# Attention with a new written order: other durations in the planner, padded queries in weight memory, eleven exp buffers

## The chip, the cores and the metric

One NeuronCore of one Trainium2 chip runs the whole program. The metric is the device time of one execution in microseconds (us). The kernel before took 1060.55 us, the median of three runs (1060.35 to 1061.62).

Engines: TensorE (PE, matrix products; PEld is its weight loading), VectorE (DVE), ScalarE (ACT), GpSimd (POOL), SyncE (SP, which here only issues DMAs). All work on SBUF; results of TensorE land in PSUM.

## The reference, cut to what matters

Three layers follow each other. The change touches the first one only.

```
q, k rotated by position (RoPE), batch 4, heads 8, seq 576, head_dim 64
scores = q k^T / 8 ; attn = softmax(scores) ; y = attn v        (fp32)
x = y as 2304 rows of 512
x = (sigmoid(x wg) * (x wv)) wo                                 (gated layer, 512 -> 1536 -> 512)
expert of each row by argmax of its logits; x = p * (relu(x w1[e]) w2[e])   (8 experts)
```

## The kernel before, in words

**Pairs and tiles.** Two heads are worked on together: 16 pairs `p`, each with nine tiles `t` of 128 query rows (four for each head and one that holds the last 64 rows of both heads); `T = 9 p + t`. All products are done with a number split into a high and a low part of the type fp32r, and the products of the parts added.

**One pair.** `plan_loads` (L321) loads raw q and raw k with their half-swapped copies (`sa<-in_qk`, L328), one DMA for q (half 0) and one for k (half 1), and `v` (L338). `plan_prep` (L418) prepares pairs 2 to 15: multiply by the cosine and sine tables for a half ("rope", L162, 128 x 1152), add the two products ("rot", L160), copy out the high part ("hi", L152 on ScalarE or L154 on GpSimd), subtract it to get the low part ("lo", L437), and then 14 DMAs (`cp`, L455) bring the parts into the layout that the products need: `q2`, `kh` (in tile `sb`), `qd` and `qz`. `qz` is the "padded query": the high part of one head's queries with the other 64 partitions zero. Pairs 0 and 1 take another way (`plan_direct`, L358), mostly without DMAs.

The raw tile and the tile of the parts (both in `sa`) exist once. So the load of a half for pair p+1 waits for "lo" of pair p, "hi" of pair p+1 waits for all copies of pair p, and "lo" of pair p also waits for the last scores of pair p-2, whose place it takes (`q2`, `kh`, `kl`, `qz` exist twice).

**One tile** (`plan_tile`, L474): scores on TensorE into PSUM ("s", L183, two PSUM tiles); VectorE copies them out to an exp buffer `e` and takes the row minimum ("tsa", L193); ScalarE does the exponential in place with the row sum (L205); TensorE transposes it (L237); ScalarE copies the high part out ("hi" of the tile, `pth`, L267) and VectorE the low part (`ptl`, L271). `transpose5` (L252) does the last 64 columns for several tiles at once. An exp buffer comes free when both transposes of its tile are done; there are `E_BUFS = 8`. Four times a pair the products with `v` follow ("value", L284), a copy by ScalarE (`xv`, L292) and an add by VectorE (`xy`, L301). Once a pair the reciprocal row sums go through DRAM (`rw`, L498; read back by `recip_rows`, L226) and the result is normalised ("rm", `normalise`, L231). The reads of pair p wait for "rm" of pair p-1.

**What sets the order.** Every instruction of attention is added to a `Plan` with an engine, a cost in us, what it depends on and a due time. `Plan.order` (L52) runs through time: the engine that can start first takes, of what is ready by the plan's own account, the operation with the lowest due time. `LAT` is added to the end of an operation until another engine sees it. All DMAs together are one engine "DMA" that does one transfer after the other, and each has an issue on "SP" (0.62 us below a size of 0.5, else 0.46) ahead of it. What results is the fixed program order of each engine: on the chip an engine waits at the head of its queue when what it needs isn't there, even where later work is ready. The due times are the tables `PR` (preparation) and `OFF` (tiles); the tables `LO`, `VLO`, `ROPE`, `RM`, `HI`, `VHI` name the pairs whose operation of that kind runs on another engine than usual (usual: low part of q or k on VectorE, low part of v on GpSimd, rope and rot on GpSimd, normalisation on GpSimd, high parts on ScalarE).

**Around it.** While attention runs, the three matrices of block 0 of the gated layer's weights are converted from double words (`filler`). `Gated.early` (L726) starts the first gate products in attention's PSUM, and `Gated.opening` makes a plan of its own from the plan's last times. `add_weights` (L624) makes the tiles for converted weights: index 0 and 1 (tag `wr`) before attention, 2 and 3 after it. During attention index 0 is filled; of index 1 only parts are used by `early`, at the end.

Of the kernel before, what the change touches and what calls it, by code (L numbers as in the profile page):

```python
# [8 lines left out]
F32R = mybir.dt.float32r  # L9
# [12 lines left out]
TPP = 9  # L22
E_BUFS = 8
PT_BUFS = 3
# [7 lines left out]
class Plan:  # L32
# [3 lines left out]

    LAT = {"PE": 0.25, "SP": 0.65, "DMA": 1.0}

# [68 lines left out]
class Attention:  # L107
    def __init__(self, tc, pool, xpool, psum_s, psum_t, psum_v, qk, v, rope, ident, xt, rows):
# [12 lines left out]
        self.kl = [t([128, S], F32R, f"kl_{i}") for i in range(2)]  # L121
        self.qd = [t([128, 128], F32R, f"qd_{i}") for i in range(2)]
        self.qz = [t([128, 2, 512], F32R, f"qz_{i}") for i in range(2)]
        sa = xpool.tile([128, 7 * S], F32R, name="sa", tag="sa", bufs=1)
        self.raw = f32(sa[:, 0:4 * S]).rearrange("p (a s) -> p a s", a=4)
        self.hqk = sa[:, 4 * S:7 * S].rearrange("p (a s) -> p a s", a=3)
        self.hq, self.hk = self.hqk[:, 0:2], self.hqk[:, 2]
        sb = xpool.tile([128, 4 * S + 4 * 640], F32R, name="sb", tag="sb", bufs=1)
        kh = sb[:, 0:4 * S].rearrange("p (i x s) -> p i x s", i=2, x=2)
        q2 = sb[:, 4 * S:].rearrange("p (i x s) -> p i x s", i=2, x=2)  # L130
        self.q2, self.kh = ([a[:, i] for i in range(2)] for a in (q2, kh))
        self.xv = t([128, 320], F32, "xv")
# [53 lines left out]
    def evac_scores(self, T):  # L186
        ps = self.s.pop(T)
        e = self.pool.tile([128, 2, SH], F32, name="e", tag="e", bufs=E_BUFS)
        p, t = divmod(T, TPP)
        if t == 0:  # L190
            self.stat[p] = self.pool.tile([128, 3, TPP], F32, name="st", tag="st", bufs=ST_BUFS)
# [129 lines left out]
    def plan_loads(self, p, load_rope=None, load_const=None):  # L321
# [8 lines left out]
        for half in (1, 0) if p == 0 else (0, 1):  # L330
            for n, cols in enumerate(self.cuts(p, half)):
                size = 1.64 * (cols.stop - cols.start) / S
                self.dma(("load", p, half, n), size, ld(half, cols), [("lo", p - 1, half)], at)
                if p == 0 and half == 1:
                    self.dma(("rope", n), size, lambda cols=cols: load_rope(cols), [], at)
        if p == 0:
            self.dma("const", 1.05, load_const, [], at)
        self.dma(("loadv", p), 0.82, lambda: nc.sync.dma_start(out=self.vraw, in_=self.v[b, hp]), [("vlo", p - 1)], at)  # L338

    def plan_v(self, p):  # L340
# [4 lines left out]
        eng = self.VHI.get(p, "ACT")  # L345
        self.op(("vhi", p), eng, {"ACT": 0.57, "POOL": 0.72}[eng], lambda eng=eng: self.copy(eng, vv[:, :, 0], self.vraw),
                [("loadv", p)] + prev, pr)
        eng = self.VLO.get(p, "POOL")
        self.op(("vlo", p), eng, {"DVE": 0.669, "POOL": 1.36}[eng], lambda: self.engine(eng).tensor_tensor(
            out=vv[:, :, 1], in0=self.vraw, in1=f32(vv[:, :, 0]), op=ALU.subtract), [("vhi", p)], pr)  # L350
# [7 lines left out]
    def plan_direct(self, p, pr):  # L358
# [7 lines left out]
        for half in (1, 0):  # L366
            j = 2 * half
            for n, c in enumerate(self.cuts(p, half)):
# [21 lines left out]
                for x in range(2):  # L390
                    last = min(c.stop, 512) if x else c.stop
                    cuts = [(c.start, last, 0)] + ([(512, S, 64)] if last < c.stop else [])
                    for a, b, d in cuts:
# [9 lines left out]
                        if a < 512:  # L403
                            if p > 0:
                                self.dma(("qz", *key), 0.4, lambda x=x, i=slice(a, min(b, 512)): nc.sync.dma_start(
                                    out=f32(self.qz[p][r[x], x, i]), in_=f32(q2[r[x], x, i])), [("qhi", *key)], pr + 1.5 + x + n)
# [11 lines left out]
    def plan_prep(self, p):  # L418
# [6 lines left out]
        for j, off in ((0, 0.0), (2, self.PR["k"])):  # L425
# [4 lines left out]
            c = {"DVE": 0.5, "POOL": 1.0}[eng]  # L430
            self.op(("rope", p, j), eng, 2.57 * c, lambda j=j, eng=eng: self.rope_op(eng, j, "both"), [("load", p, half, 0)], base + off)
            self.op(("rot", p, half), eng, 1.36 * c, lambda j=j, eng=eng: self.rope_op(eng, j, "add"), [("rope", p, j)], base + off)
# [4 lines left out]
            self.op(("lo", p, half), eng, {"DVE": 0.669, "POOL": 1.36}[eng], lambda j=j, hi=hi, lo=lo, eng=eng: self.engine(eng).tensor_tensor(  # L437
                out=lo, in0=raw[:, j], in1=f32(hi), op=ALU.subtract), [("hi", p, half)] + before, base + off + self.PR["split"])
# [15 lines left out]
        for n, (half, o, s) in enumerate(cp):  # L454
            self.dma(("cp", p, n), 0.4 if n < 2 or half else 0.2, lambda o=o, s=s: dma(out=f32(o), in_=f32(s)),  # L455
                     [("lo", p, half)] + before, base + 3 * half + 2)
# [7 lines left out]
    KLO = ((0, 0, 0), (0, 1, 1), (1, 0, 0),)  # L464
    LO = dict.fromkeys(((3, 0), (4, 0), (4, 1), (5, 0), (5, 1), (6, 0), (6, 1), (7, 0), (7, 1), (9, 0), (9, 1), (10, 0), (10, 1), (11, 1), (12, 0), (12, 1), (13, 0), (13, 1), (14, 0), (15, 0), (15, 1),), "POOL")
    VLO = dict.fromkeys((1, 5, 8, 13,), "DVE")
    ROPE = dict.fromkeys(((1, 1),), "DVE")
    PR = dict(ahead=-0.74, k=-25.57, split=-30.40, v=-9.46)
    RM = dict.fromkeys((8, 10, 15,), "DVE")
    HI = dict.fromkeys(((2, 0), (3, 0), (3, 1), (5, 1), (7, 1), (8, 1), (11, 1), (12, 1), (14, 0),), "POOL")  # L470
    VHI = dict.fromkeys((0, 2, 3, 11, 12, 14, 15,), "POOL")
    OFF = dict(table=-3.16, xs=781.16, gv=847.57, post=751.36, rr=85.85, rm=56.64, s=11.92, tsa=14.25, exp=3.09, eps=-75.21, rec=-94.73, norm=-14.47, tr=79.75, hi=4.82, lo=18.38, tr5=-12.17, val=102.41, vc=-0.58, va=-66.51)

# [21 lines left out]
    def plan_norm(self, p):  # L495
# [4 lines left out]
        for x, part in reads:  # L500
            self.dma(("rr", p, x, part), 0.1 if part else 0.36, lambda x=x, part=part: self.recip_rows(p, x, part),
                     [("rw", p), ("rm", p - 1)], T + o["rr"])
        eng = self.RM.get(p, "POOL")
        self.op(("rm", p), eng, {"DVE": 0.67, "POOL": 1.36}[eng], lambda: self.normalise(p, eng),
                [("rr", p, *k) for k in reads] + [("va", p, *k) for k in reads], T + o["rm"])
# [28 lines left out]
    def plan_value(self, p, x, u):  # L534
# [11 lines left out]
    def run(self, npairs=B * NP, loads=(None, None), filler=(), tail=None):  # L546
# [64 lines left out]
class Gated:  # L611
# [196 lines left out]
    def opening(self):  # L808
# [65 lines left out]
        def convert(seq, prio, step, free):  # L874
            for n, (f, m) in enumerate(seq):
                dep = [(*seq[n - 2], 5)] if n > 1 else []
                for i, (eng, cost, fn) in enumerate(self.convert(f, m, nc.sync.dma_start)):
# [738 lines left out]
def build(tc, qk, v, rope, cst_in, wg, wv, wo, wg2, bias, mod, w1, w2, out):  # L1616
# [5 lines left out]
    with tc.manual_schedule(), pool("keep") as keep:  # L1622
        cst = keep.tile([128, CSTW], F32, name="cst", tag="cst")
        ident = cst[:, CST["ident"]]
        with pool("wa") as wa:
            with pool("xy") as xyp, pool("conv") as conv, pool("xs") as xs:
                xy = xyp.tile([128, KC, NT], F32, name="xy", tag="xy")
                gated = Gated(tc, words(wg), words(wv), words(wo), xy, wa, conv, xs, ident)
                with pool("att") as att, \
# [48 lines left out]
```

## Time and profile before

| | |
|---|---|
| median of 3 runs | 1060.55 us |
| profiled execution | 1062.35 us, of it 1060.5 us span |
| busy over the span | PE 94%, DVE 63%, ACT 50%, POOL 36% |
| attention | 0 to about 335 us |
| gated layer, routing, experts | after it, to the end |

An engine's busy time is the sum of its instructions' spans; PE's is modelled. A wait is named after what ended it. "SPq" is SyncE's DMA queue, and a DMA in the chain of waits is the time from its issue until what waited for it went on.

### The profile page before, as it was taken

The page shows a single profiled execution, that of the slowest core. Times are in us where ns is not written, and L with a number is a line of the kernel's source. Part 1 is how long each engine was busy: PE and PEld are TensorE (multiplying, and loading weights), DVE is VectorE, ACT ScalarE, POOL GpSimd, SP SyncE. Part 2 cuts the span into 40 slices and gives each one's busy share as a digit, 9 for nine tenths or more (in the row PEclk, how much of TensorE's full clock was granted, in tenths as well). Part 3 has the DMA queues.
Part 4 walks back from the last instruction along what each step waited for, and adds up shares of the span by engine and source line. Part 5 has one row for each costly group of instructions (what it writes and reads, how often), then busy time and mean ns, then how long its engine had stood idle before and what let it go on. Part 6 is the DMA issues. An engine that isn't in the chain of part 4 may idle for free.

```text
span 1060.5 us, 16517 instructions
## 1 busy us (share of the span) xinstructions
PE 994.1 (94%) x6035; PEld 912.6 (86%) x6035; DVE 664.0 (63%) x1179; ACT 532.9 (50%) x1051; POOL 386.3 (36%) x288
## 2 busy tenths in 40 slices
PE   3988889889899999999999999999998899999996
PEld 2888888889899999999999999998875799999995
DVE  8999788879796764544535545532267755555651
ACT  5878787879796622222222212233331554555552
POOL 5788766778520532322322323211142111211111
PEclk9999999999999999999999999999998999999998
DMA  5567766577511320111111101000027867666640
GB/s 190 164 180 185 169 190 165 151 191 199 152 45 52 109 71 22 60 40 40 41 40 40 60 21 60 20 1 1 1 61 233 295 233 233 225 225 220 222 170 24
DMA packets 74137, 127.24 MB, mean 120 GB/s; under 512 B 14447, under 2 KB 37631, under 8 KB 74048
## 3 DMA queue, kind: packets, MB, share of 16 engines
q1 hardware_dynamic: 60128, 108.53, 34.6%
q0 software_dynamic: 3040, 9.70, 2.7%
q10 hardware_dynamic: 10880, 7.87, 2.4%
q8 instruction: 50, 0.82, 0.3%
q14 instruction: 39, 0.32, 0.1%
HBM read 95.65 MB, written 9.77 MB: 99 GB/s over the span
## 4 chain that ended last, share of the span: by engine, by line
PE 52%; issue 17%; DMA 12%; DVE 9%; ACT 4%; POOL 3%; SPq 2%; ACTq 0%; POOLq 0%; DVEq 0%
PE gv L715 28%; PE yo L781 13%; DMA out<-e_y,r_si 5%; DMA sa<-in_qk 4%; PE pv L284 3%; DMA sb<-sa 3%; PE s L183 3%; DVE e L193 2%; SPq L455 2%; PE pt L237 2%; DVE ptl L271 1%; ACT e L205 1%; POOL e_xg L1446 1%; ACT pth L267 1%; PE s L715 1%
## 5 line engine op out<-in xcount | busy, mean ns | idle before, releaser
L724 POOL TENSOR_TENSOR gl<-sg,gh 128x384 fp32r<-128x384 f32 x60 | 64.2, 1070 | 263.3 <-ACT gh L723 263.3
L722 DVE TENSOR_TENSOR sg<-gv,sg 128x384 f32<-128x384 f32 x70 | 39.0, 557 | 140.9 <-PE gv L715 118.9
L205 ACT ACTIVATE e<-e,st 128x576 f32<-128x576 f32 x144 | 112.1, 782 | 8.3 <-DVE e L193 7.5
L1439 DVE TENSOR_TENSOR e_w<-wr,e_w 128x1024 fp32r<-128x1024 f32 x80 | 95.9, 1222 | 28.9 <-ACT e_w L1438 27.1
L183 PE MATMUL s<-sb 128*128 128x288 f32 x320 | 78.1, 335 | 33.5 <-DVE sb L398 14.0
L193 DVE TENSOR_SCALAR_CACHE_REDUCE e<-s 128x576 f32<-128x576 f32 x144 | 105.6, 745 | 2.6 <-PE s L183 2.0
L721 ACT ACTIVATE sg<-gv 128x384 f32<-128x384 f32 x70 | 34.3, 490 | 140.1 <-PE gv L715 140.0
L271 DVE TENSOR_TENSOR ptl<-pt,pth 128x512 fp32r<-128x512 f32 x144 | 94.2, 680 | 8.2 <-ACT pth L267 7.2
L1438 ACT CAST e_w<-wr 128x1024 fp32r<-128x1024 f32 x80 | 81.4, 1047 | 23.9 <-DMA x_rows<-xy 19.8
L162 POOL TENSOR_TENSOR sa<-sa,rope 128x1152 f32<-128x1152 f32 x28 | 75.0, 2679 | 45.0 <-DMA sa<-in_qk 39.7
L1494 PE MATMUL e_py<-e_w,e_hh 128*128 128x512 f32 x288 | 89.7, 393 | 0.0
L183 PEld LDWEIGHTS s<-sb 128*128 128x128 f32 x320 | 51.0, 199 | 44.5 <-DVE e L193 21.4
L237 PE MATMUL pt<-cst,e 128*128 128x128 f32 x576 | 83.0, 280 | 5.3 <-DVE ptl L271 5.2
L1509 POOL DMA_INDIRECT out<-e_y,r_si x19 | 19.6, 1030 | 187.2 <-ACT e_y L1508 187.2
L267 ACT CAST pth<-pt 128x512 fp32r<-128x512 f32 x144 | 79.4, 588 | 7.7 <-PE pt L237 6.5
L1476 PE MATMUL e_ph<-e_xh,e_w 128*128 128x256 f32 x576 | 81.9, 286 | 0.7 <-ACT e_xh L1459 0.7
L723 ACT CAST gh<-sg 128x384 fp32r<-128x384 f32 x60 | 30.8, 514 | 101.1 <-DVE sg L722 101.0
L284 PE MATMUL pv<-pth,vv 128*128 128x256 f32 (+1 forms) x256 | 76.0, 318 | 3.3 <-DVE xy L301 2.7
L715 PE MATMUL gv<-xe,wb 128*128 128x384 f32 x384 | 78.9, 338 | 0.0
L1476 PEld LDWEIGHTS e_ph<-e_xh,e_w 128*128 128x128 f32 x576 | 75.7, 194 | 1.5 <-ACT e_xh L1459 0.9
L237 PEld LDWEIGHTS pt<-cst,e 128*128 128x128 f32 x576 | 68.7, 144 | 8.8 <-DVE ptl L271 4.5
L715 PE MATMUL gv<-xh,wb 128*128 128x384 f32 x288 | 74.1, 338 | 0.0
(245 smaller groups left out, 2497.6 us busy)
## 6 DMA issues: line engine op xcount, KB each, us to landing
wr<-in_w SPq DMA_DIRECT2D x74, 512.0 KB
sa<-in_qk SPq DMA_DIRECT2D x30, 576.0 KB
sb<-sa SPq DMA_DIRECT2D x84, 144.0 KB
wraw<-in_wg SPq DMA_DIRECT2D x12, 512.0 KB
wraw<-in_wv SPq DMA_DIRECT2D x12, 512.0 KB
wraw<-in_wo SPq DMA_DIRECT2D x12, 512.0 KB
vraw<-in_v SPq DMA_DIRECT2D x16, 320.0 KB
x_rows<-xy ACTq DMA_DIRECT2D x18, 256.0 KB
```

The lines of the kernel that those rows point to most:

```text
L183: nc.tensor.matmul(ps[:, u, 0:SH], a, m[:, SH * u:SH * u + SH], start=n == 0, stop=n == len(mm) - 1)
L193: self.nc.vector.tensor_scalar(out=e, in0=ps[:, :, 0:SH], scalar1=-0.125, scalar2=3.0e38, op0=ALU.mult, op1=ALU.min, accum_out=st[:, 0])
L205: nc.scalar.activation(out=e, in_=e, func=AF.Exp, bias=st[:, 0], scale=-1.0, accum_out=st[:, 1])
L237: nc.tensor.transpose(pt[:, c], e[:, 128 * c:128 * c + 128], self.ident)
L267: self.nc.scalar.copy(out=hi, in_=src)
L271: self.nc.vector.tensor_tensor(out=lo, in0=src, in1=f32(hi), op=ALU.subtract)
L284: nc.tensor.matmul(ps[:, 0:w], a, m, start=n == 0, stop=n == len(mm) - 1)
L715: self.nc.tensor.matmul(p[:, 0:U], a[:, wc], b[:, c], start=c == 0 and n == 0, stop=c == KC - 1 and n == 2)
L781: nc.tensor.matmul(ps, a, b, start=n == 0, stop=n == 3 * len(GROUPS[grp]) - 1)
L1439: nc.vector.tensor_tensor(out=lo, in0=raw, in1=f32(hi), op=ALU.subtract)
L1476: nc.tensor.matmul(ps[:, k], a[:, fs], b[:, c], start=n == 0, stop=n == 3 * KC - 1)
L1494: nc.tensor.matmul(ps, a[:, f, hs], b, start=n == 0, stop=n == 23)
```

## The change

- The two padded query tiles `qz` are no longer tiles of attention's pool. They are the first two weight tiles of index 1 (`Gated.idle`), each 128 x 2 x 512.
- `E_BUFS` is 11 instead of 8. The tile of a pair's row statistics is made by the first tile of the pair that is evacuated, whichever it is.
- The planner's durations are others: DMAs cost more (a load 2.2 instead of 1.64 and `LAT` 2.0 instead of 1.0, copies 0.55 and 0.3 instead of 0.4 and 0.2, `v` 1.22 instead of 0.82), several operations on GpSimd and ScalarE a little more.
- The tables of engines and due times are others.

```diff
-E_BUFS = 8
+E_BUFS = 11
-    LAT = {"PE": 0.25, "SP": 0.65, "DMA": 1.0}
+    LAT = {"PE": 0.25, "SP": 0.65, "DMA": 2.0}
...
-        self.qz = [t([128, 2, 512], F32R, f"qz_{i}") for i in range(2)]
+        self.qz = qz
...
-        if t == 0:
+        if p not in self.stat:
             self.stat[p] = self.pool.tile([128, 3, TPP], F32, name="st", tag="st", bufs=ST_BUFS)
...
-                size = 1.64 * (cols.stop - cols.start) / S
+                size = 2.2 * (cols.stop - cols.start) / S
...
-            self.dma("const", 1.05, load_const, [], at)
-        self.dma(("loadv", p), 0.82, lambda: ...
+            self.dma("const", 1.42, load_const, [], at)
+        self.dma(("loadv", p), 1.22, lambda: ...
...
-        self.op(("vhi", p), eng, {"ACT": 0.57, "POOL": 0.72}[eng], ...
+        self.op(("vhi", p), eng, {"ACT": 0.62, "POOL": 0.76}[eng], ...
-        self.op(("vlo", p), eng, {"DVE": 0.669, "POOL": 1.36}[eng], ...
+        self.op(("vlo", p), eng, {"DVE": 0.74, "POOL": 1.58}[eng], ...
...
-            self.op(("rope", p, j), eng, 2.57 * c, ...
-            self.op(("rot", p, half), eng, 1.36 * c, ...
+            self.op(("rope", p, j), eng, 2.64 * c, ...
+            self.op(("rot", p, half), eng, 1.43 * c, ...
-            self.op(("lo", p, half), eng, {"DVE": 0.669, "POOL": 1.36}[eng], ...
+            self.op(("lo", p, half), eng, {"DVE": 0.669, "POOL": 1.43}[eng], ...
-            self.dma(("cp", p, n), 0.4 if n < 2 or half else 0.2, ...
+            self.dma(("cp", p, n), 0.55 if n < 2 or half else 0.3, ...
...
-    LO = dict.fromkeys(((3, 0), (4, 0), (4, 1), (5, 0), (5, 1), (6, 0), (6, 1), (7, 0), (7, 1), (9, 0), (9, 1), (10, 0), (10, 1), (11, 1), (12, 0), (12, 1), (13, 0), (13, 1), (14, 0), (15, 0), (15, 1),), "POOL")
-    VLO = dict.fromkeys((1, 5, 8, 13,), "DVE")
-    ROPE = dict.fromkeys(((1, 1),), "DVE")
-    PR = dict(ahead=-0.74, k=-25.57, split=-30.40, v=-9.46)
-    RM = dict.fromkeys((8, 10, 15,), "DVE")
-    HI = dict.fromkeys(((2, 0), (3, 0), (3, 1), (5, 1), (7, 1), (8, 1), (11, 1), (12, 1), (14, 0),), "POOL")
-    VHI = dict.fromkeys((0, 2, 3, 11, 12, 14, 15,), "POOL")
-    OFF = dict(table=-3.16, xs=781.16, gv=847.57, post=751.36, rr=85.85, rm=56.64, s=11.92, tsa=14.25, exp=3.09, eps=-75.21, rec=-94.73, norm=-14.47, tr=79.75, hi=4.82, lo=18.38, tr5=-12.17, val=102.41, vc=-0.58, va=-66.51)
+    LO = dict.fromkeys(((4, 0), (4, 1), (5, 0), (6, 0), (6, 1), (7, 1), (8, 0), (8, 1), (9, 1), (11, 1), (12, 0), (12, 1), (14, 1), (15, 0), (15, 1),), "POOL")
+    VLO = dict.fromkeys((9, 14,), "DVE")
+    ROPE = dict.fromkeys(((1, 0), (1, 1), (2, 0), (6, 0),), "DVE")
+    PR = dict(ahead=-5.46, k=-139.78, split=-159.58, v=-65.53)
+    RM = dict.fromkeys((0, 1, 2, 4, 5, 6, 7, 10, 12, 15,), "DVE")
+    HI = dict.fromkeys(((2, 0), (2, 1), (3, 0), (5, 0), (6, 0), (6, 1), (7, 1), (8, 0), (9, 1), (10, 1), (11, 0), (12, 1), (13, 0), (14, 0), (14, 1), (15, 0),), "POOL")
+    VHI = dict.fromkeys((1, 2, 4, 8, 9, 10,), "POOL")
+    OFF = dict(table=0.16, xs=728.99, gv=822.87, post=977.12, rr=92.46, rm=165.62, s=-46.75, tsa=13.27, exp=86.93, eps=-141.16, rec=-185.35, norm=-135.21, tr=37.99, hi=46.49, lo=16.94, tr5=-62.52, val=70.55, vc=-103.28, va=-328.79)
...
-            self.dma(("rr", p, x, part), 0.1 if part else 0.36, ...
+            self.dma(("rr", p, x, part), 0.1 if part else 0.5, ...
-        self.op(("rm", p), eng, {"DVE": 0.67, "POOL": 1.36}[eng], ...
+        self.op(("rm", p), eng, {"DVE": 0.67, "POOL": 1.43}[eng], ...
-        self.op(("vc", p, x, u), "ACT", 0.065 + w / 960, ...
+        self.op(("vc", p, x, u), "ACT", 0.11 + w / 960, ...
...
+            if i == 1:
+                self.spare = w[0:2]
...
+    def idle(self):
+        return self.spare
...
-                        op(("cv", f, m, "dma"), "DMA", 1.46, lambda: None, [("cv", f, m, 0)], 0)
+                        op(("cv", f, m, "dma"), "DMA", 1.95, lambda: None, [("cv", f, m, 0)], 0)
```

## Rows read from the trace of the kernel before

**Rows 1.** Stretches: from:to, length, busy us (instructions) PE, PEld, DVE, ACT, POOL, PEclk, DMA, GB/s

```profile
50.00:100.00 50.00, 44.01 (x320) 41.14 (x319) 46.37 (x100) 40.89 (x97) 41.30 (x27) 0.97 0.69 178
90.00:281.00 191.00, 167.81 (x1238) 157.81 (x1239) 158.33 (x362) 155.91 (x362) 138.51 (x85) 0.98 0.68 175
283.00:314.50 31.50, 31.00 (x246) 29.90 (x245) 29.64 (x73) 29.93 (x73) 8.31 (x6) 1.00 0.28 75
337.00:700.00 363.00, 362.73 (x1919) 340.71 (x1919) 193.53 (x289) 109.00 (x207) 105.34 (x91) 1.00 0.15 46
```

**Rows 2.** Score evacuation: group of 90 to 281 us; stretch 283 to 314.5 (two instructions a tile)

```profile
L193 DVE TENSOR_SCALAR_CACHE_REDUCE e<-s 128x576 f32<-128x576 f32 x91 | 66.8, 745 | 1.1 <-PE s L183 0.8 <-PE pt L237 0.2
...
283.00:314.50 31.50, 13.14 (x36) 1.00 0.28 75
```

**Rows 3.** Chain of waits, 90 to 281 us, shares of the stretch

```profile
by line: DMA sa<-in_qk 20.4%; DMA sb<-sa 14.9%; SPq L455 9.4%; PE pv L284 6.6%; PE s L183 6.0%; issue 5.5%; DVE e L193 4.3%; ACT e L205 4.1%; ACT pth L267 3.4%; PE pt L237 2.9%; DVE ptl L271 2.7%; POOL kl L437 2.5%; ACT xv L292 2.1%; ACT sa
```

**Rows 4.** SyncE in order of time: start us, us, queue line operation, tiles, count

```profile
96.07 0.36 SPq L328 DMA_DIRECT2D sa<-in_qk  x1
...
132.60 0.33 SPq L328 DMA_DIRECT2D sa<-in_qk  x1
...
134.24 0.54 SPq L328 DMA_DIRECT2D sa<-in_qk  x1
...
149.25 2.38 SPq L226 DMA_DIRECT2D rr<-recip_rows  x4
...
261.02 0.33 SPq L328 DMA_DIRECT2D sa<-in_qk  x1
```

**Rows 5.** GpSimd in order of time, idle time before in brackets

```profile
131.15 1.43 POOL L437 TENSOR_TENSOR kl<-sa 128x576 fp32r<-128x576 f32 x1 [0.63 <-PE s L183]
...
136.88 2.67 POOL L162 TENSOR_TENSOR sa<-sa,rope 128x1152 f32<-128x1152 f32 x1 [2.69 <-DMA sa<-in_qk]
139.50 1.55 POOL L349 TENSOR_TENSOR vv<-vraw,vv 128x640 fp32r<-128x640 f32 x1
...
143.08 2.67 POOL L162 TENSOR_TENSOR sa<-sa,rope 128x1152 f32<-128x1152 f32 x1 [0.63 <-DMA sa<-in_qk]
145.71 1.44 POOL L231 TENSOR_TENSOR xy<-xy,rr 128x576 f32<-128x576 f32 x1
149.60 0.68 POOL L154 TENSOR_SCALAR sa<-sa 128x576 fp32r<-128x576 f32 x1 [2.45 <-DMA sb<-sa]
150.24 1.42 POOL L160 TENSOR_TENSOR sa<-sa 128x576 f32<-128x576 f32 x1
```

**Rows 6.** Groups of 90 to 281 us: shapes xcount | busy us, mean ns | idle before, releasers

```profile
L162 POOL TENSOR_TENSOR sa<-sa,rope 128x1152 f32<-128x1152 f32 x20 | 53.4, 2671 | 31.6 <-DMA sa<-in_qk 31.6
L160 POOL TENSOR_TENSOR sa<-sa 128x576 f32<-128x576 f32 x22 | 32.0, 1463 | 0.2
...
L152 ACT CAST sa<-sa 128x576 fp32r<-128x576 f32 x16 | 10.8, 673 | 20.9 <-POOL sa L160 8.6 <-DMA sb<-sa 5.5 <-issue 3.6
...
L349 DVE TENSOR_TENSOR vv<-vraw,vv 128x640 fp32r<-128x640 f32 x3 | 3.6, 1215 | 0.0
L437 DVE TENSOR_TENSOR kl<-sa 128x576 fp32r<-128x576 f32 x2 | 2.8, 1384 | 2.3 <-POOL sa L154 1.9 <-ACT sa L152 0.4
L437 DVE TENSOR_TENSOR sa<-sa 128x576 fp32r<-128x576 f32 x2 | 2.6, 1320 | 0.5 <-ACT sa L152 0.5
L231 DVE TENSOR_TENSOR xy<-xy,rr 128x576 f32<-128x576 f32 x2 | 2.3, 1142 | 0.0
```

**Rows 7.** VectorE in order of time: two low parts

```profile
150.31 1.96 DVE L437 TENSOR_TENSOR kl<-sa 128x576 fp32r<-128x576 f32 x1 [1.89 <-POOL sa L154]
...
153.48 0.74 DVE L437 TENSOR_TENSOR sa<-sa 128x576 fp32r<-128x576 f32 x1
```

**Rows 8.** Waits, 90 to 281 us: us in total, times, longest us

```profile
DVE xy L301 <- ACT xv L292: 17.4, 14, 3.8
...
SPq L226 <- POOL xy L231: 5.3, 3, 3.0
```

More of the change, by code (lines that the diff above doesn't have):

```diff
@@ L107, with __init__ @@
 class Attention:
-    def __init__(self, tc, pool, xpool, psum_s, psum_t, psum_v, qk, v, rope, ident, xt, rows):
+    def __init__(self, tc, pool, xpool, psum_s, psum_t, psum_v, qk, v, rope, ident, xt, rows, qz):
         self.tc, self.nc = tc, tc.nc
@@ L336, in plan_loads @@
         if p == 0:
-            self.dma("const", 1.05, load_const, [], at)
-        self.dma(("loadv", p), 0.82, lambda: nc.sync.dma_start(out=self.vraw, in_=self.v[b, hp]), [("vlo", p - 1)], at)
+            self.dma("const", 1.42, load_const, [], at)
+        self.dma(("loadv", p), 1.22, lambda: nc.sync.dma_start(out=self.vraw, in_=self.v[b, hp]), [("vlo", p - 1)], at)
     def plan_v(self, p):
@@ L345, in plan_v @@
         eng = self.VHI.get(p, "ACT")
-        self.op(("vhi", p), eng, {"ACT": 0.57, "POOL": 0.72}[eng], lambda eng=eng: self.copy(eng, vv[:, :, 0], self.vraw),
+        self.op(("vhi", p), eng, {"ACT": 0.62, "POOL": 0.76}[eng], lambda eng=eng: self.copy(eng, vv[:, :, 0], self.vraw),
                 [("loadv", p)] + prev, pr)
         eng = self.VLO.get(p, "POOL")
-        self.op(("vlo", p), eng, {"DVE": 0.669, "POOL": 1.36}[eng], lambda: self.engine(eng).tensor_tensor(
+        self.op(("vlo", p), eng, {"DVE": 0.74, "POOL": 1.58}[eng], lambda: self.engine(eng).tensor_tensor(
             out=vv[:, :, 1], in0=self.vraw, in1=f32(vv[:, :, 0]), op=ALU.subtract), [("vhi", p)], pr)
@@ L404, in plan_direct @@
                             if p > 0:
-                                self.dma(("qz", *key), 0.4, lambda x=x, i=slice(a, min(b, 512)): nc.sync.dma_start(
+                                self.dma(("qz", *key), 0.5, lambda x=x, i=slice(a, min(b, 512)): nc.sync.dma_start(
                                     out=f32(self.qz[p][r[x], x, i]), in_=f32(q2[r[x], x, i])), [("qhi", *key)], pr + 1.5 + x + n)
@@ L430, in plan_prep @@
             c = {"DVE": 0.5, "POOL": 1.0}[eng]
-            self.op(("rope", p, j), eng, 2.57 * c, lambda j=j, eng=eng: self.rope_op(eng, j, "both"), [("load", p, half, 0)], base + off)
-            self.op(("rot", p, half), eng, 1.36 * c, lambda j=j, eng=eng: self.rope_op(eng, j, "add"), [("rope", p, j)], base + off)
+            self.op(("rope", p, j), eng, 2.64 * c, lambda j=j, eng=eng: self.rope_op(eng, j, "both"), [("load", p, half, 0)], base + off)
+            self.op(("rot", p, half), eng, 1.43 * c, lambda j=j, eng=eng: self.rope_op(eng, j, "add"), [("rope", p, j)], base + off)
             eng = self.HI.get((p, half), "ACT")
@@ L436, in plan_prep @@
             eng = self.LO.get((p, half), "DVE")
-            self.op(("lo", p, half), eng, {"DVE": 0.669, "POOL": 1.36}[eng], lambda j=j, hi=hi, lo=lo, eng=eng: self.engine(eng).tensor_tensor(
+            self.op(("lo", p, half), eng, {"DVE": 0.669, "POOL": 1.43}[eng], lambda j=j, hi=hi, lo=lo, eng=eng: self.engine(eng).tensor_tensor(
                 out=lo, in0=raw[:, j], in1=f32(hi), op=ALU.subtract), [("hi", p, half)] + before, base + off + self.PR["split"])
@@ L454, in plan_prep @@
         for n, (half, o, s) in enumerate(cp):
-            self.dma(("cp", p, n), 0.4 if n < 2 or half else 0.2, lambda o=o, s=s: dma(out=f32(o), in_=f32(s)),
+            self.dma(("cp", p, n), 0.55 if n < 2 or half else 0.3, lambda o=o, s=s: dma(out=f32(o), in_=f32(s)),
                      [("lo", p, half)] + before, base + 3 * half + 2)
@@ L500, in plan_norm @@
         for x, part in reads:
-            self.dma(("rr", p, x, part), 0.1 if part else 0.36, lambda x=x, part=part: self.recip_rows(p, x, part),
+            self.dma(("rr", p, x, part), 0.1 if part else 0.5, lambda x=x, part=part: self.recip_rows(p, x, part),
                      [("rw", p), ("rm", p - 1)], T + o["rr"])
         eng = self.RM.get(p, "POOL")
-        self.op(("rm", p), eng, {"DVE": 0.67, "POOL": 1.36}[eng], lambda: self.normalise(p, eng),
+        self.op(("rm", p), eng, {"DVE": 0.67, "POOL": 1.43}[eng], lambda: self.normalise(p, eng),
                 [("rr", p, *k) for k in reads] + [("va", p, *k) for k in reads], T + o["rm"])
@@ L540, in plan_value @@
                 [("lo", a) for a in ts] + [("lo", (p, u, 5)), ("vlo", p)], T + o["val"], "pv")
-        self.op(("vc", p, x, u), "ACT", 0.065 + w / 960, lambda: self.value_copy(p, x, u),
+        self.op(("vc", p, x, u), "ACT", 0.11 + w / 960, lambda: self.value_copy(p, x, u),
                 [("value", p, x, u), ("va", p - 1 + u, x, 1 - u)], T + o["vc"])
@@ L564, in run @@
                 if i == 0:
-                    self.dma(("cv", n, i), 1.46, fn, dep, 1000.0 + n)
+                    self.dma(("cv", n, i), 1.95, fn, dep, 1000.0 + n)
                 else:
@@ L1633, in build @@
                     rt = att.tile([128, 2, S], F32, name="rope", tag="rope")
-                    at = Attention(tc, att, xs, ps_s, ps_t, ps_v, qk, v, rt, ident, xy, rows)
+                    at = Attention(tc, att, xs, ps_s, ps_t, ps_v, qk, v, rt, ident, xy, rows, gated.idle())
                     at.run(loads=(lambda c: nc.sync.dma_start(out=rt[:, :, c], in_=rope[:, :, c]), lambda: nc.sync.dma_start(out=cst, in_=cst_in)),
```

## The prediction

> **What bounds the kernel now.** I read the busy times by stretch first. From 337 to 700 us TensorE is busy 362.73 of 363 us [rows 1], so a microsecond won in the attention stage ahead of it is a microsecond won at the end, and the later stages give nothing of their own. In the attention stage no engine is full: from 90 to 281 us the shares are TensorE 88%, VectorE 158.33 of 191.00 = 83%, ScalarE 82%, GpSimd 73% [rows 1]. 91 score tiles are evacuated there [rows 2], ten pairs of nine, so a pair takes 19.1 us. The last two pairs need no preparation any more, and there 18 tiles pass in 31.5 us [rows 2], 15.8 us a pair, with VectorE at 29.64 of 31.50 = 94% [rows 1].
>
> Then the chain of waits for the same 191 us: loads of raw q and k 20.4%, the copies out of the staging tile 14.9%, SyncE's queue at the copies 9.4% [rows 3]. That is 45%, 85 us, in one loop. Raw tile and split tile exist once, so: low part of pair p, load of p+1, rotation on GpSimd, high part, low part of p+1. Ten pairs of loads are issued between 96.07 and 261.02 us (nine periods in the SyncE rows, of which the first and the last stand here) [rows 4]: 18.3 us a period. That almost equals the pair time, so the loop sets the pace and VectorE, ScalarE and TensorE wait around it.
>
> One turn of the loop, event by event [rows 4, 5]: low part at 131.15, loads issued at 132.60 and 134.24, first rotation 136.88, so the first load took 4.3 us; second rotation 143.08, so the second took 8.8 us. The planner counted 0.46 + 0.65 + 1.64 + 1.0 = 3.75 us for one and 1.6 more for the second, 5.4. Because it expected the loads early, it put other work into the turn: the value's low part at 139.50 (1.55 us) between multiply and add, the normalisation at 145.71 (1.44), then a wait of 2.45 us for the copies of the pair before, at 149.60. ScalarE is hit too: its high parts stood at the head of its queue for 20.9 us, released by GpSimd's add, DMAs and issue [rows 6].
>
> By a sentence of the Trainium skill ("SBUF — State Buffer", The DMA setup-cost knee) a transfer costs about 2 us plus its bytes over 436 GB/s; that gives an estimate of 3.4 us for such a load, near the old planner's figure, and the loop would have 5 us to spare. Here two loads and the copies share the queue and the 8.8 us decides.
>
> **The change part by part.**
>
> *Durations.* The new figures give 0.46 + 0.65 + 2.2 + 2.0 = 5.3 us for one load and 7.5 for the second, against 4.3 and 8.8. So the written order now expects the loads about when they come, and fillers and high parts can stand where they wait for nothing. The two fillers (3.0 us) and part of the 2.45 us wait can leave the turn: 18.3 becomes 15 to 16 us at best. If the loop alone counted, that would be 25 to 33 us over ten pairs. It does not: something else is late next.
>
> *Work moved to VectorE*, counted from the tables for the pairs prepared in 90 to 281 us: five more low parts, four more normalisations (six pairs of ten instead of two), one value low part less, and for pair 6 one double multiply and one add. All read two SBUF operands. One that waits for nothing takes 0.74 us [rows 7], so 5 x 0.74 + 4 x 0.74 - 0.8 + (1.35 + 0.74) = 7.9 us; the double multiply of 1152 columns isn't in the trace on VectorE and is taken as 2 x 0.74 less one start, 1.35, with bounds 0.74 and GpSimd's 2.67 [rows 6]. But the nine such operations of this stretch took 2.8 + 2.6 + 3.6 + 2.3 = 11.3 us [rows 6], 1.26 each: one that begins while GpSimd runs, as at 150.31 beside GpSimd's add of 150.24, took 1.96 [rows 5, 7]. Ten more of them at 0.5 us of excess cost 5.0. VectorE goes from 158.3 to 171.2 us, 17.1 a pair.
>
> *GpSimd* loses five low parts and four normalisations at about 1.43 [rows 5], a multiply of 2.67 and an add of 1.46 [rows 6], and gains seven high parts at 0.68 (149.60) and a value low part of 1.55: about -10.7 us of 138.5, off the path already, but out of the loop. ScalarE loses seven high parts of 0.67, -4.7 of 155.9, and with them part of its 20.9 us at the head of the queue.
>
> *First four pairs.* There VectorE takes on one low part, three normalisations, a double multiply and an add, less one value low part: 0.74 + 2.2 + 2.1 - 0.8 = 4.2 us, and 5 x 0.5 of excess, 6.7. From 50 to 100 us VectorE is busy 46.37 of 50 [rows 1], so little hides it. Bounds 0 and 6.7; the stretch before 50 us has gaps, I take 2.
>
> *Eleven exp buffers, padded queries in weight memory.* The same memsets and copies run; only addresses differ. VectorE's waits for a buffer, told by transposes, are 0.2 us [rows 2], so directly the buffers give 0 to 0.2 us. What they do is let the order run scores further ahead: the new due times put scores before transposes and values. The price of that is inside the utilisation below. The weight tiles used are those of block 1, converted only after attention, so no write waits; if one did, TensorE's rows from 337 us on would show it.
>
> *Other edits.* The statistics tile is made by whichever tile comes first: nothing. The later conversions are reordered by 1.95 for 1.46, beside a TensorE with 0.27 us of idle in 363: nothing; without that cover one conversion's half microsecond. Normalisation now has a late due time, and the reads of the next reciprocals wait for it in SyncE's queue ahead of loads and copies; this wait is 5.3 us already [rows 8]. I add nothing and keep it for the range, 0 to 5.
>
> *The sum.* With the loop at 16 us or less VectorE is late next. At the 94% of the last two pairs, 171.2 / 0.94 = 182 us for what took 191: -9. The first pairs +2. Together -7, from the profiled run's 1062.35 us (span 1060.5 and 1.85 around it) to 1055.3; that run lies 1.8 above the median, so against 1060.55 it is **1053.5 us**.
>
> **The rivals.**
>
> *VectorE becomes the bound without being filled: slower.* With 171.2 us of work the stage breaks even at 171.2 / 191 = 89.6% busy; below it the change loses. For it: the stage stands at 83%; VectorE waits 17.4 us for ScalarE's value copies [rows 8], which no duration of a DMA explains; VectorE's figures in the planner still leave out the 0.5 us of excess. At 87%, midway from today to the tail, 197 us: +6, with +2 early, 1068.5. Against it: 46.37 of 50 was reached with preparation running. The Trainium skill ("SBUF — State Buffer", Who interferes with whom) says that VectorE and GpSimd hold a shared port pair as an exclusive lock, and a two-operand VectorE instruction blocks fully behind a GpSimd one that reads SBUF. The 1.96 us row agrees; if each of the ten hit the start of a rotation instead, 2.7 us each in place of 0.5, it would be 22 us more and the same side.
>
> *The loop stays at 18.3 us.* Second load 8.8, rotation and add 4.1, high and low part 2.1 make 15.0 us with nothing between them, and the 14 copies of the pair before must have landed ahead of the next high part: at about 0.6 us of issue each (four reads took 2.38 [rows 4]) 8.4 us of SyncE's queue that no new duration shortens. If both together already need the 18.3, then the pair time stays, 1058 to 1063.
>
> *TensorE becomes the bound.* If the run-ahead fills every gap, pairs go at 16.5 to 17.3 us, toward the 15.8 of the tail, where TensorE is at 31.00 of 31.50. VectorE would need 99% with 17.1, so I allow 17.3: -18, 1042.
>
> **How the numbers follow.** Forecast 0.50 (1047 to 1058), slower 0.22, loop unchanged 0.15, TensorE 0.13. The range 1041 to 1066 leaves out the lower half of the last and a good half of the slower one. A difference of 0.2%, 2.1 us, is what can be told from none. Faster: 0.48 of the forecast, 0.13 and 0.02 of the unchanged loop, 0.63. Same 0.13, of it 0.11 the unchanged loop. Slower 0.24.
>
> **What would show it.** Right: periods of the loads under 18 us, no value low part and no normalisation between multiply and add on GpSimd, ScalarE's head-of-queue wait at the high parts well under 20.9 us, and the first full TensorE stretch some 7 us earlier. VectorE's two-operand operations should rise from 9 to about 19 in the ten pairs at 1.1 to 1.3 us each, and its share to 94%. Wrong: VectorE under 90% with longer waits for ScalarE; or SyncE standing at the reciprocal reads for more than 10 us; or loads still 18 us apart.

## The result and the profile after

The changed kernel takes 1049.72 us, the median of four runs (1049.16 to 1051.54), beside 1060.94 us for the kernel before, run with it: ratio 0.9897, 95% interval 0.988 to 0.9914, 11.2 us less. The profiled execution took 1049.16 us, its span 1046.8.

The gain lies in attention and nowhere else. Attention's last value product ends at 317.8 us instead of 332.2; from there to the end it is 729.0 us, before 728.3. Inside attention there are two parts of opposite sign:

| stretch | before | after |
|---|---|---|
| start to the last score evacuation of pair 3 | 90.2 us | 95.6 us |
| from there to the last evacuation of pair 13 (ten pairs) | 191.2 us | 171.4 us |
| from there to the last value product | 50.8 us | 50.8 us |

The boundaries are evacuations, and the two orders differ in what TensorE has done by then. Up to the first boundary, before and after (columns as in [rows 1]):

```profile
0.00:90.20 90.20, 68.58 (x422) 59.87 (x422) 82.86 (x169) 67.08 (x154) 64.94 (x45) 0.98 0.65 181
```

```profile
0.00:95.60 95.60, 73.73 (x449) 63.76 (x449) 89.32 (x176) 70.48 (x161) 58.24 (x44) 0.98 0.63 176
```

The changed kernel has 27 more products behind it there (transposes counted), so part of its 5.4 us more is work done earlier, and part of the 19.8 us less is owed to that. The sum, 14.4 us at the end of attention, doesn't depend on it.

The stretches of the profile after: the first pairs, the same window of time as before and the gated layer; below them the ten pairs.

```profile
55.00:95.00 40.00, 35.51 (x251) 32.79 (x250) 39.59 (x78) 31.77 (x75) 27.70 (x18) 0.96 0.67 171
...
90.00:281.00 191.00, 180.62 (x1365) 169.65 (x1364) 185.20 (x408) 166.00 (x388) 134.26 (x83) 1.00 0.71 182
...
337.00:700.00 363.00, 363.00 (x1941) 341.30 (x1940) 186.08 (x282) 102.95 (x202) 102.48 (x91) 1.00 0.14 44
```

```profile
95.60:267.00 171.40, 162.26 (x1228) 152.51 (x1227) 167.51 (x368) 149.71 (x351) 127.54 (x78) 1.00 0.73 189
```

VectorE, 83% busy before, is at 167.51 of 171.40, 97.7%. The chain of waits over 90 to 268 us answers to [rows 3]. The loop of loads, copies and SyncE's queue was 45% of it before. Now loads are 3.9%, and neither the copies nor SyncE's queue at them reach 1.5%; VectorE's two big operations lead.

```profile
by line: DVE e L193 18.3%; DVE ptl L271 15.3%; PE s L183 12.0%; PE pv L284 10.8%; issue 8.2%; PE pt L237 7.6%; DVE xy L301 4.1%; DMA sa<-in_qk 3.9%; DVE xy L231 2.2%; DVE p5l L271 2.1%; DMA rr<-recip_rows 1.6%; POOL sa L162 1.5%; ACT e L205
```

Two turns on GpSimd answer to [rows 5]. Between a multiply (L162) and the adds (L160) no value low part (L349) and no normalisation (L231) stands any more; they come after the high and low parts or while the next load is under way. The first-issued loads of the ten pairs go out between 93.77 and 253.53 us, nine periods of 17.8 us, before 18.3 [rows 4]. The nine together are only 5.2 us shorter.

```profile
204.52 2.68 POOL L162 TENSOR_TENSOR sa<-sa,rope 128x1152 f32<-128x1152 f32 x1 [1.24 <-DMA sa<-in_qk]
208.79 2.67 POOL L162 TENSOR_TENSOR sa<-sa,rope 128x1152 f32<-128x1152 f32 x1 [1.59 <-DMA sa<-in_qk]
211.42 3.29 POOL L160 TENSOR_TENSOR sa<-sa 128x576 f32<-128x576 f32 x2
216.84 1.44 POOL L437 TENSOR_TENSOR sa<-sa 128x576 fp32r<-128x576 f32 x1 [2.12 <-ACT sa L152]
218.25 0.67 POOL L154 TENSOR_SCALAR sa<-sa 128x576 fp32r<-128x576 f32 x1
219.00 1.44 POOL L437 TENSOR_TENSOR kl<-sa 128x576 fp32r<-128x576 f32 x1
220.37 1.57 POOL L349 TENSOR_TENSOR vv<-vraw,vv 128x640 fp32r<-128x640 f32 x1
222.86 2.63 POOL L162 TENSOR_TENSOR sa<-sa,rope 128x1152 f32<-128x1152 f32 x1 [0.92 <-DMA sa<-in_qk]
```

The groups of 90 to 268 us answer to [rows 6]: VectorE's two-operand operations, ScalarE's high parts, and the adds behind ScalarE's value copies.

```profile
L301 DVE TENSOR_TENSOR xy<-pv,xv 64x320 f32<-64x320 f32 x21 | 10.2, 485 | 0.5
L231 DVE TENSOR_TENSOR xy<-xy,rr 128x576 f32<-128x576 f32 x6 | 9.9, 1646 | 0.1
...
L437 DVE TENSOR_TENSOR sa<-sa 128x576 fp32r<-128x576 f32 x6 | 6.4, 1063 | 0.0
...
L152 ACT CAST sa<-sa 128x576 fp32r<-128x576 f32 x7 | 4.7, 676 | 3.9 <-POOL sa L160 2.5 <-DMA sb<-sa 1.4
...
L437 DVE TENSOR_TENSOR kl<-sa 128x576 fp32r<-128x576 f32 x3 | 2.2, 742 | 0.0
...
L349 DVE TENSOR_TENSOR vv<-vraw,vv 128x640 fp32r<-128x640 f32 x1 | 1.8, 1811 | 0.0
...
L162 DVE TENSOR_TENSOR sa<-sa,rope 128x1152 f32<-128x1152 f32 x1 | 1.4, 1350 | 0.0
L160 DVE TENSOR_TENSOR sa<-sa 128x576 f32<-128x576 f32 x1 | 0.8, 755 | 0.0
```

Eighteen two-operand operations where there were nine, 22.5 us where it was 11.3: 1.25 us each as before. Their waits behind GpSimd are counted as busy (the last section has the rows), so part of the 97.7% is waiting. ScalarE's head-of-queue wait at the high parts went from 20.9 to 3.9 us, and the 17.4 us that VectorE waited for value copies [rows 8] are gone (0.5 in the row of L301).

### The profile page after: what moved, and what is told of

Read it like the earlier page. It is cut to its first block, busy times and chain, and to the rows that moved or that the text cites. A ratio compares the mean times of both kernels' runs of the same rounds, so it can differ in the third digit from the quotient of the medians.

```text
span 1046.8 us, 16540 instructions
## 1 busy us (share of the span) xinstructions
PE 994.3 (95%) x6035; PEld 910.9 (87%) x6035; DVE 680.7 (65%) x1194; ACT 530.6 (51%) x1045; POOL 367.8 (35%) x279
## 4 chain that ended last, share of the span: by engine, by line
PE 52%; issue 18%; DVE 16%; DMA 8%; POOL 3%; ACT 3%; SPq 0%; POOLq 0%; DVEq 0%; ACTq 0%
PE gv L721 28%; PE yo L787 13%; DMA out<-e_y,r_si 5%; DVE e L193 5%; DVE ptl L271 4%; PE pv L284 3%; PE s L183 3%; PE pt L237 2%; POOL e_xg L1452 1%; DVE xy L301 1%; ACT e L205 1%; PE s L721 1%; DMA sb<-sa 1%; PE r_pl L1221 1%; PE r_pt L1185 1%
## 5 line engine op out<-in xcount | busy, mean ns | idle before, releaser
L205 ACT ACTIVATE e<-e,st 128x576 f32<-128x576 f32 x144 | 112.3, 782 | 21.2 <-DVE e L193 20.5
L1500 PE MATMUL e_py<-e_w,e_hh 128*128 128x512 f32 x288 | 89.6, 392 | 0.0
L162 POOL TENSOR_TENSOR sa<-sa,rope 128x1152 f32<-128x1152 f32 x26 | 69.5, 2674 | 37.1 <-DMA sa<-in_qk 29.6
L284 PE MATMUL pv<-pth,vv 128*128 128x256 f32 (+1 forms) x256 | 73.9, 311 | 5.8 <-DVE xy L301 4.1
```

The source lines that it names most:

```text
L205: nc.scalar.activation(out=e, in_=e, func=AF.Exp, bias=st[:, 0], scale=-1.0, accum_out=st[:, 1])
L284: nc.tensor.matmul(ps[:, 0:w], a, m, start=n == 0, stop=n == len(mm) - 1)
L1500: nc.tensor.matmul(ps, a[:, f, hs], b, start=n == 0, stop=n == 23)
```

## The experiments

Each ran beside the kernel before; ratios are to it, with the 95% interval. The experiments ran in three groups on three chips, and runs of the kernel before ranged over some 8 to 11 us in each, so differences between groups under half a per cent are not read from ratios or medians. The row under each is one stretch of its profile in the columns of [rows 1]: from the last evacuation of pair 3 to the last value product. For the two kernels themselves it is:

```profile
90.20:332.20 242.00, 218.47 (x1617) 207.07 (x1618) 200.46 (x457) 197.85 (x460) 149.34 (x92) 0.98 0.59 155
```

```profile
95.60:317.80 222.20, 211.68 (x1591) 199.67 (x1590) 210.11 (x464) 191.45 (x448) 137.34 (x85) 1.00 0.64 167
```

### More work for VectorE, before and after

```diff
+        if t in (4, 8):    # the same evacuation once more
+            self.nc.vector.tensor_scalar(out=e, in0=ps[:, :, 0:SH], ...)
```

> The kernel before, in which VectorE evacuates two of the nine score tiles of every pair twice (same instruction, same result): 32 more instructions of 0.675 us pitch, 21.6 us of VectorE, order else unchanged. Theory (the preparation loop at 18.3 us a period paced the kernel before, VectorE stood at 83% with some 32 us idle in ten pairs): most of it is taken up by VectorE's idle time, +3 to +10 us. Rival (VectorE's queue was the pace in the kernel before too, its idle time being waits that nothing else fills): +16 to +22 us.

> The same 32 doubled evacuations in the changed kernel. Theory (VectorE at 98% between 90 and 268 us is the bound now): +17 to +22 us on 1049.7. Rival (the pace is still the loop or TensorE, and VectorE is only busy beside it): +10 us or less.

```profile
94.30:338.00 243.70, 219.14 (x1611) 203.80 (x1611) 219.18 (x507) 199.38 (x460) 146.50 (x90) 0.99 0.59 153
```

```profile
99.70:333.70 234.00, 215.86 (x1591) 199.86 (x1590) 222.93 (x516) 193.22 (x448) 137.06 (x85) 1.00 0.61 158
```

The kernel before went to 1.0079 (1.0047 to 1.0112), +8.4 us, as the theory had it. The stretches begin with the first of pair 3's two last evacuations, so 25 of the 32 extra ones, 16.9 us, fall into each; before, it takes 1.7 us more. The changed kernel went to 1.0047 (1.0026 to 1.0068), against its own 0.9897 some +16 us, just under the 17 to 22 expected; there the stretch takes 11.8 us more, with VectorE's busy time 12.8 us higher. VectorE was beside the pace before and is nearly at it now. No run adds work to TensorE, so what share it has in the pace is not tested.

### Half the load, before and after

```diff
+            if p > 1:
+                cols = slice(0, SH)
             return lambda: nc.sync.dma_start(out=self.raw[:, h, cols], in_=self.qk[b, hp, :, h, cols])
```

> The kernel before, in which the loads of raw q and k of pairs 2 to 15 bring columns 0 to 287 only, half the bytes; the other columns keep what was there. Order unchanged. Theory (the landing of the loads is part of the loop that paces): the second load comes some 2 to 3 us sooner, the period falls toward 16 us, -8 to -20 us. Rival (loads aren't in the pace; the copies or VectorE's queue are): -3 to 0 us.

> The same halved loads in the changed kernel. Theory (the loads have slack there, VectorE is full): -2 to 0 us. Rival (the loop still paces, only with a shorter period): -5 us or more.

```profile
91.80:318.00 226.20, 212.65 (x1611) 201.89 (x1611) 203.71 (x457) 196.69 (x460) 147.15 (x89) 1.00 0.52 138
```

```profile
97.00:314.70 217.70, 210.74 (x1592) 199.62 (x1589) 207.19 (x466) 190.85 (x448) 138.10 (x85) 1.00 0.55 143
```

Before: 0.9879 (0.9838 to 0.992), -12.8 us, and the stretch 15.8 us shorter with the order untouched: the loads, or the copies that share the queue with them, paced it. The loads' period fell from 18.3 to 17.1 us, not to 16. After: 0.9818 (0.9771 to 0.9865), by the ratios some 8 us and by the medians 6.4 us under the changed kernel, where 0 to 2 were expected: the rival's number came. The profiled run is the slowest of its four (1047.46 of 1040.23 to 1047.46). It shows 4.5 us in the stretch, of which VectorE's own busy time gives 2.9, and 1.2 us in the span. So the loads are not out of the pace after the change; what the rest of the 8 us is stays open.

### Buffers, durations, due times, engines: one after the other

```diff
 # bufs11: E_BUFS, the padded queries and the statistics tile of the change, nothing else
 # bufs11_new_durations: that and the planner's durations of the change
 # old_engines: the changed kernel with LO, VLO, ROPE, RM, HI, VHI of before
 # old_durations: the changed kernel with the durations of before
```

> The kernel before with eleven exp buffers and the padded queries in weight memory, and nothing else: durations, tables and due times of before. Theory (the loop paces; buffers don't shorten it): -3 to +2 us on the kernel before. Rival (run-ahead is what was missing): -5 to -11 us.

```profile
89.40:350.90 261.50, 227.30 (x1621) 213.90 (x1620) 205.56 (x459) 198.23 (x460) 149.43 (x92) 0.95 0.56 143
```

> The kernel before with eleven buffers and the new durations, tables and due times of before. Theory (durations free the loop by themselves): -4 to -10 us on the kernel before, the loads' period under 17.8 us. Rival (only together with the new due times): -2 to +5 us.

```profile
104.20:335.80 231.60, 214.29 (x1614) 202.52 (x1613) 201.72 (x454) 196.40 (x458) 145.47 (x89) 1.00 0.63 163
```

> The changed kernel with the engine tables of before (low parts, value low parts, normalisation, rotation, high parts); durations, due times and buffers as changed. VectorE loses 12 to 19 us of work in the whole, GpSimd gets it. Theory (VectorE is the bound and the moves to it were no help): 1040 to 1050 us. Rival (GpSimd stands in the loop, and taking work from it freed the loop): pairs 4 to 13 take over 175 us, 1052 to 1062 us.

```profile
96.20:320.10 223.90, 213.59 (x1616) 202.77 (x1615) 199.08 (x454) 195.97 (x458) 150.81 (x91) 1.00 0.63 167
```

> The changed kernel with the planner's durations of before; tables, due times, eleven buffers and padded queries as changed. Theory (with the true durations the order puts fillers and high parts where the loads have come; that is what freed the loop): waits at the head of ScalarE's and GpSimd's queues come back, pairs 4 to 13 take 180 us or more instead of 171, 1055 to 1068 us. Rival (tables and run-ahead do it, whatever the durations): 1046 to 1053 us.

```profile
102.70:354.60 251.90, 224.87 (x1608) 209.90 (x1607) 214.98 (x465) 193.76 (x453) 136.39 (x84) 0.96 0.57 148
```

Eleven buffers alone: 1.0224 (1.0182 to 1.0266), 24 us slower, which neither theory had. The plan is made anew with them. Why the new plan is slower is not shown: copies rise from 14.9% to 20.5% of the chain between 90 and 281 us, but loads fall from 20.4% to 7.0%, and 9.1 of the 19.5 us that the stretch grows come after pair 13. Part may be TensorE's granted clock: its mean over the stretch is 0.95, for 0.98 in the kernel before. The new durations on top: 0.9999 (0.9972 to 1.0026). The total missed my -4 to -10 and is the rival's number; the loads' period, 17.6 us, and the stretch, 261.5 to 231.6 us, are the theory's. The first pairs lose 14.8 of it again (pair 3 ends at 104.2). The new due times on top: 0.9955 (0.9933 to 0.9977); pair 3 ends at 96.2 and the stretch takes 223.9. Last the engines, which makes the changed kernel: 0.9897, measured in another group.

Taken the other way, the changed kernel with old durations: 1.0201 (1.016 to 1.0242), stretch 251.9. The direction is the theory's (pairs 4 to 13 take 196 us, and ScalarE stands idle 21.7 us ahead of its high parts again), but its 1055 to 1068 was too low: the median is 1083. No step of this row but the last two gets ahead of the kernel before; together they bring the gain, and only with the new durations. The new durations with the eight buffers of before were not run, so what they give without the buffers stays open.

The engine tables are the part on which my theory failed: taking work back from VectorE gave no 1040 to 1050. The ten pairs were faster, 167.3 us, but from pair 13 to the last value product it took 56.6 instead of 50.8, with more of TensorE's products left for it (403 for 366 in the changed kernel).

### What VectorE waits for GpSimd

```diff
+    def one(self, out, in_):
+        self.nc.vector.tensor_scalar(out=out, in0=in_, scalar1=1.0, scalar2=3.0e38, op0=ALU.mult, op1=ALU.min, accum_out=self.sink)
...
+        if eng == "DVE":    # normalise; the low parts of q and k likewise, from the high part
+            return self.one(x, self.rr[p])
```

> The changed kernel, in which the 13 low parts of q and k and the ten normalisations that run on VectorE read one SBUF operand instead of two (a copy with a running minimum, the form of the score evacuation; the subtraction and the multiplication are left out). Order and waits as changed. In the profile these 23 took 8.9 us longer together than at 0.745 us each. Theory (they wait for a GpSimd instruction that is running, and VectorE is full): -5 to -9 us on 1049.7. Rival (what they wait is found again as another wait of VectorE, or comes from somewhere else than GpSimd): -2 to 0 us.

```profile
92.40:310.50 218.10, 209.74 (x1590) 199.53 (x1589) 204.30 (x480) 190.93 (x448) 133.49 (x85) 1.00 0.66 167
```

Its whole time, 1.0204 (1.0152 to 1.0255), can't be compared: other values send rows to other experts (21 gathers instead of 19), and after attention it took 772 us instead of 729. Attention is unaffected by that, and ends at 310.5 instead of 317.8 us: -7.3, inside the theory's -5 to -9. The 23 operations took 0.74 us each now, beside a GpSimd that was busy as before (133 us for 137 in the stretch): the 8.9 us of waits are gone from them.

But the order of waits did not stay as changed. A low part that doesn't read the raw tile no longer holds up the next load, which now goes out behind the high part. The same load (q of pair 12) and the low part ahead of it, in the changed kernel and in this run:

```profile
198.91 0.74 DVE L437 TENSOR_TENSOR sa<-sa 128x576 fp32r<-128x576 f32 x1
199.68 0.33 SPq L328 DMA_DIRECT2D sa<-in_qk  x1
```

```profile
194.73 0.33 SPq L334 DMA_DIRECT2D sa<-in_qk  x1
195.89 0.74 DVE L158 TENSOR_SCALAR_CACHE_REDUCE sa<-sa 128x576 fp32r<-128x576 f32 x1
```

Thirteen low parts lie ahead of a load in this way, and the halved loads showed that earlier loads help. So the 7.3 us are what the waits and the earlier loads are worth together; no run separates them.

### Three tries for a better one

```diff
-    RM = dict.fromkeys((0, 1, 2, 4, 5, 6, 7, 10, 12, 15,), "DVE")
+    RM = {}                       # rm_pool
 # mixed: engine tables of before for pairs 4 to 13, of the change for the others
-E_BUFS = 11
+E_BUFS = 9                        # bufs9
```

> The changed kernel with all sixteen normalisations on GpSimd (ten of them on VectorE in the changed one, 13.2 us there); the plan orders anew. Theory (VectorE is the bound, GpSimd has room): -4 to -10 us on 1049.7, VectorE between pairs 4 and 13 under 96%. Rival (GpSimd's 1.43 us each stand in the preparation loop again): 0 to +8 us.

```profile
95.00:317.70 222.70, 210.37 (x1592) 199.80 (x1591) 202.29 (x456) 190.39 (x447) 143.34 (x91) 1.00 0.63 166
```

> The changed kernel with the engine tables of before for pairs 4 to 13, where the run with all tables of before took 167 us against 171, and those of the change for the other pairs, where it lost 6 us after pair 13. Theory (in the middle VectorE is the bound and the moves to it cost, at the end they help): 1043 to 1047 us. Rival (the loss at the end came from the order of the middle): 1050 to 1057 us.

```profile
92.20:323.80 231.60, 215.07 (x1611) 203.48 (x1610) 204.82 (x461) 196.53 (x460) 146.17 (x88) 0.99 0.62 161
```

> The changed kernel with nine exp buffers instead of eleven (eight cannot be planned with the new due times). Theory (the new due times run scores ahead, and need the buffers; buffers by themselves were no help, 22 us the other way, with the old ones): +4 to +20 us on 1049.7. Rival (the gain is the durations' and tables' alone): -2 to +3 us.

```profile
98.70:319.40 220.70, 210.96 (x1595) 199.60 (x1594) 203.86 (x464) 190.95 (x448) 134.08 (x83) 1.00 0.64 164
```

None beats the changed kernel: 0.9947 (0.9916 to 0.9979), 0.9944 (0.9922 to 0.9966), 0.9941 (0.9917 to 0.9966). Without normalisations VectorE has 7.8 us less to do in the stretch, and it takes 222.7 us instead of 222.2. The ten pairs and what comes after them, and the latter in the changed kernel:

```profile
95.00:261.30 166.30, 156.57 (x1196) 148.66 (x1194) 156.10 (x356) 145.71 (x344) 130.46 (x82) 1.00 0.74 193
261.30:317.70 56.40, 53.80 (x396) 51.14 (x397) 46.20 (x101) 44.68 (x104) 12.89 (x10) 1.00 0.31 87
```

```profile
267.00:317.80 50.80, 49.41 (x366) 47.16 (x365) 42.60 (x97) 41.74 (x98) 9.80 (x8) 1.00 0.34 93
```

The ten pairs end 5.7 us sooner, with VectorE at 94%, as the theory had it, but 30 more of TensorE's products are left for the end, which takes 5.6 us more. So less work for VectorE did move the middle; the new order gave it back. That TensorE, at 95% of the stretch in the changed kernel and 94% here, holds the end where it is would explain it and isn't shown; with one operand it reached 96%. By the ratio the kernel is some 5 us slower, the rival's 0 to 8. Its ten runs lay between 1048.3 and 1060.5, and the profiled one is the fastest of them; what the others lose stays open. The mixed tables again lose at the end (57.7 us after pair 13, 407 products), and their ten pairs took 173.9 us, not 167: the time is the rival's, and the loss at the end comes with the order of the middle. With nine buffers the profile differs by the first pairs, +3.1, less 1.5 in the stretch; the ratio would say +4.6 us, across groups. The buffers' share is small or unsettled.

## Why the prediction was right

The forecast was 1053.5, the time is 1049.7, inside the range, and the mechanism is in the main the one named: the planner's durations loosen the loop, and VectorE is late next. Two terms were mis-sized in opposite directions, so that the total came so close is partly luck. Term by term:

- **The loop paced the kernel before.** Shown: halved loads take 15.8 us from the stretch, 16.9 us of extra VectorE work add 1.7.
- **Durations free it.** Shown in kernels with eleven buffers: 261.5 to 231.6 us with them, 222.2 to 251.9 without. They do it through the order only, and with the due times made for them.
- **The loop at 16 us or less** did not come. Its period is 17.8 us, 5.2 of the 19.8 us over nine turns, and just under the 18 that was named as the sign. GpSimd still waits 17.6 us for loads between 90 and 268 us (31.6 before [rows 6]), and halved loads still gain. The loop is shorter and mostly hidden, not gone.
- **VectorE's added work, +12.9 us to 171.2.** It is 167.5, +9.0. Number and price of the operations were right, 18 for 19 and 1.25 for 1.26 us.
- **VectorE's share, 94%, was the term mis-sized most.** It came to 97.7%. With 167.5 at 94% the ten pairs would have taken 178.2 us, with 171.2 182; they took 171.4. So -9 was -19.8. I had taken the share of the last two pairs as what an order can reach, and those are TensorE's pairs (31.00 of 31.50 [rows 1]).
- **First pairs, +2 with bounds 0 and 6.7**: +5.4, near the upper bound. VectorE's busy time there rose by 6.5 us; pair 2's rotation is 2.1 of that, and one low part of pair 1 behind GpSimd took 4.68 us where it had taken 1.85: 2.8. Part of the +5.4 is TensorE's work done earlier.
- The two misses partly cancel: -19.8 + 5.4 is -14.4 at the end of attention, -13.2 between the profiled runs and -11.2 between the medians.
- **The slower rival** needed VectorE under 89.6%; it didn't come. Its price was there, 0.5 us for each of the 18 operations, and is paid inside the gain. By the Trainium skill ("SBUF — State Buffer", Who interferes with whom) a VectorE instruction with at most one SBUF input, outside the 2-port modes, does not contend with GpSimd. The trace agrees: the 23 one-operand forms took 0.74 us each.
- **TensorE as the bound** was nearer than its 0.13: the pair time, 17.1 us, lies in its 16.5 to 17.3, with TensorE at 162.26 of 171.40 us. That VectorE and not TensorE sets the pace rests on the doubled evacuations, and they cost 11.8 us for 16.9, not all of it.
- **SyncE at the reciprocal reads**: not shown as a loss; the reads stand in the chain with 1.6%, and SyncE's waits there for work on `xy` sum to 2.6 us between 90 and 268 us, before 5.3 [rows 8].

## What to carry to other kernels

In an order written out by hand or by a planner, a transfer's assumed duration is a decision about whose queue stands still: correct these first, from the trace, before searching for priorities: with the old ones more buffers made the kernel 24 us slower, with the new ones they cost nothing. Before pricing a change that loads an engine, double some of that engine's work: 16.9 us for 1.7 says that it has room, 16.9 for nearly 12 that it has little. An experiment that leaves out an operand also takes away the waits that hang on it; look in the trace whether something else now starts sooner. Where two orders are compared up to a boundary, count the work that each has left behind it. An order is one thing: buffers alone gave +2.2%, buffers and durations 0%, everything together -1%.

## What the runs showed of the hardware

A VectorE instruction with two SBUF operands can wait for a running GpSimd instruction, and the wait counts as its busy time. In the changed kernel twelve low parts, normalisations and a value low part took over 0.95 us. Each began while a GpSimd instruction ran and ended 0.6 to 0.7 us after that one's end. The longest of them began 0.2 us after GpSimd's multiply of 208.79:

```profile
208.99 3.09 DVE L231 TENSOR_TENSOR xy<-xy,rr 128x576 f32<-128x576 f32 x1
```

It ended at 212.08, 0.62 us after the multiply, although GpSimd's next instruction had begun at 211.42, before the multiply's end. One other instruction, a low part of pair 1, stood behind four GpSimd instructions. VectorE's row, then GpSimd's:

```profile
27.02 4.68 DVE L383 TENSOR_TENSOR kl<-sa,sb 64x576 fp32r<-64x576 f32 x1
```

```profile
26.26 1.40 POOL L160 TENSOR_TENSOR sa<-sa 128x576 f32<-128x576 f32 x1
27.63 0.71 POOL L154 TENSOR_SCALAR vv<-vraw 128x640 fp32r<-128x640 f32 x1
28.33 1.26 POOL L681 TENSOR_TENSOR wr<-wt,wr 128x512 fp32r<-128x512 f32 x1
29.55 1.53 POOL L349 TENSOR_TENSOR vv<-vraw,vv 128x640 fp32r<-128x640 f32 x1
```

It began at 27.02 and ended 0.62 us after 31.08, when GpSimd paused: 4.1 us of waiting. Why this one stood behind all four and the others behind one stays open; that GpSimd's instructions overlap by some hundredths of a microsecond is the same in both.

TensorE's granted clock fell to half (1.2 of 2.4 GHz) for 3.4 us at a time after stretches in which TensorE had paused; before the change four times in attention, after it once. One of them in the kernel before, the stretch ahead and the fall (columns as in [rows 1]):

```profile
108.00:115.00 7.00, 3.67 (x28) 3.22 (x28) 3.18 (x8) 3.32 (x8) 4.40 (x4) 1.00 0.50 139
115.00:118.40 3.40, 3.40 (x16) 3.40 (x16) 2.66 (x8) 2.86 (x8) 1.70 (x2) 0.50 0.81 215
```

How much of the 14.4 us is clock no run separates. An estimate of the most: three falls fewer, 3.4 us each at half the clock, are 5.1 us if TensorE alone had set the pace there.
